# A sparse-attention and expert kernel on one core: a new written-out order, the first pair's block as one transfer, three table products on another engine

## The chip, the cores and the metric

The kernel runs on one core of a Trainium2 chip. The metric is the device time of one execution in microseconds (us), as the median of several runs: 202.86 us before the change (three runs, 202.06 to 202.98).

The core has five engines with a queue each: TensorE (PE in the profile, its weight loads PEld), VectorE (DVE), ScalarE (ACT), GpSimd (POOL) and SyncE (SP). SyncE issues nearly all DMA transfers here. Each engine works its own queue strictly in the order in which the program was written, and waits for the others by semaphores.

## The reference

Attention over 4 batches, 8 heads, 768 positions and 64 columns, followed by a soft mixture of 8 experts over the 3072 tokens. A position sees the first 8 keys and the 96 keys up to its own; the rest is masked, and a bias grows with the distance.

```python
scores = scale * np.matmul(q, k.transpose(0, 1, 3, 2))
keep = is_global | is_local
bias = -slopes[:, None, None] * dist[None, :, :]
scores = np.where(keep, scores + bias, -1000000000.0)
a = softmax(scores); x = np.matmul(a, v)          # x as (3072, 512)
...
logits = x @ phi                                  # 32 slots
d = softmax(logits, axis 0); slot_input = d.T @ x
slot_out[e] = np.maximum(slot_input[e] @ w1[e], 0) @ w2[e]
out = softmax(logits, axis 1) @ slot_out
```

(Softmax is written out in the reference, with a maximum taken off and 1e-9 added to each sum.)

## The kernel before

**Tiling.** A unit is one batch and a pair of heads: 16 units, numbered 0 to 15. Queries and keys of a unit come as one block of 128 partitions by 1664 values (832 KB, `load_qk`), its values as 448 KB (`load_v`). The 768 keys are cut into seven blocks of 120 with the 8 global keys ahead of each, and a block is multiplied with at most 216 queries, so that a score tile is keys by queries. The seven blocks go in three groups through two PSUM tiles: `scores(u, k)` writes tile (3u + k) modulo 2, for both heads.

**The steps of a unit.** `biased(u, k)` on VectorE (line 544) adds the bias table to a score tile, writes it to SBUF and keeps the running maximum. `max_t` and `max_r` (lines 551, 556) turn that into one number for the unit. `exponential(u, i)` on ScalarE (line 560) handles one head. The weights are then split into two 16-bit halves: `w_hi` (ScalarE, line 563) casts, and `w_lo` (line 570) subtracts the cast from the original, in three parts a head, either on GpSimd or, as `w_lo_dve`, on VectorE. The values are split the same way: `v_hi` on GpSimd (line 503), `v_hi_act` on ScalarE (506) or `v_hi_dve` on VectorE (509), and `v_lo` on VectorE (513). `values(u, i)` is 39 matmuls (line 587) of halves by halves. `ev_sums`, `ev_recs` and `ev_mul` divide by the row sums, `tr` transposes the result, `tr_copy` (ScalarE, 629) or `tr_copy_dve` (VectorE, 633) brings it to SBUF, and `logits` multiplies with phi. Every fourth unit ends a batch, with a few steps on its logits.

**The bias table.** The four head pairs need four tables of 1728 values in 16 bit. `table_even` (264), `table_odd` (268) and `table_rest` (273, three copies) make the first; `table_pair(p)` (280) makes table p by multiplying the first with 0.25 to the p. `biased(u, k)` of unit u reads table u modulo 4.

**The order.** Nothing is scheduled by the compiler. `ORDER` (line 51) is a list of steps written out by a planner, 608 of them, and lines 841 and 842 issue them one after the other. A step's place against others on the same engine is its place in that engine's queue. `warm` steps are matmuls on constants whose result nobody reads. The list also has the loads: `piece`, `extra` and `free` bring the experts' weights into ten tiles of their own, into gaps of the attention's tiles, and into those tiles as they come free.

```python
for name, u, *args in ORDER:
    steps[name](u, *args)
```

**Behind the attention.** `last_dispatch`, the two halves of the hidden layer (line 106), the projections (139) and the combination (199) run in a fixed order that is not in `ORDER`.

Of the kernel before, what the change touches and what calls it, by code (L numbers as in the profile page):

```python
# [15 lines left out]
AF = mybir.ActivationFunctionType  # L16
# [5 lines left out]
B, H, S, D = 4, 8, 768, 64  # L22
# [7 lines left out]
QW = KB + WIN  # L30
# [9 lines left out]
KW = NJ * KR  # L40
KCOL = tuple(KR * ((j + 5) % NJ) for j in range(NJ))
Q1 = KB + QW
# [9 lines left out]
NP = H // 2  # L52
# [157 lines left out]
class BiasTable:  # L210
# [58 lines left out]

    def rest(self):  # L270
        t = self.tabs[0]
        for at, n in ((2 * QW, QW), (3 * QW, QN[5]), (3 * QW + QN[5], QN[6])):
            self.nc.vector.tensor_copy(out=t[:, :, at:at + n], in_=t[:, :, QW:QW + n])

    def unit(self, p, k):

        return self.tabs[p][:, :, QW * k:QW * k + BW]

    def pair(self, p):
        self.nc.vector.tensor_scalar(out=self.tabs[p], in0=self.tabs[0], scalar1=0.25 ** p, scalar2=None, op0=ALU.mult)  # L280


@with_exitstack
def tile_attention_moe(ctx: ExitStack, tc: tile.TileContext, qk, v, phi, w1, w2, nn, out):
    nc = tc.nc
    const = ctx.enter_context(tc.tile_pool(name="const", bufs=1))
    fast = ExitStack()
    keep = fast.enter_context(tc.tile_pool(name="keep", bufs=1))
    wk = fast.enter_context(tc.tile_pool(name="wk", bufs=2))
    att = ExitStack()  # L290
    ap = att.enter_context(tc.tile_pool(name="ap", bufs=1))
    banks = ExitStack()
    psx = banks.enter_context(tc.tile_pool(name="psx", bufs=1, space=PSUM))
# [35 lines left out]
    rq = [r[:, 0:S + KW] for r in raws]  # L329
# [3 lines left out]
    def rqs(u):  # L333
        return EARLY[u][0][:, 0:S + KW] if u in EARLY else rq[u % 2]

    def vraws(u):
        return (EARLY[u][1] if u in EARLY else vt[:, VC * (u % 2):VC * (u % 2) + VC]).rearrange(by_head, j=NJ, i=2)
# [18 lines left out]
    held = []  # L356
    for name, i, *_ in ORDER:
        if name == "free":
# [4 lines left out]
    for k, n in enumerate(held):  # L363
        at = 0
        for c0, c1 in sorted(c for h, *cs in spaces for c in cs if h == n) + [(WP, WP)]:
            if at < c0:
                extras.append((NW + k, at, c0))
            at = c1
    places += places[0:5] + places[9:9 + 27 - npl]

    def piece(k):
        m, r = divmod(k, 16)
        if m == 0:
            a, r = divmod(r, 8)
            half, s = divmod(r, 4)
        else:
            half, r = divmod(r, 8)
            a, s = divmod(r, 4)
        return m, 4 * a + s, half
# [3 lines left out]
    def load_w(pieces, c0=0, c1=WP):  # L383

        for k in pieces:
            m, e, half = piece(k)
            nc.sync.dma_start(out=places[k][:, c0:c1], in_=(w1, w2)[m][e][:, WP * half + c0:WP * half + c1])

    def piece_of(k):
        load_w([k])  # L390

    def free(i):
        n, *cs = spaces[i]
        for c0, c1 in cs:
            load_w([NW + held.index(n)], c0, c1)

    FIRST = slice(KCOL[0], KW + Q1)

    def load_qk0(u):
        nc.sync.dma_start(out=rq[0][:, FIRST], in_=qk[0, 0][:, FIRST])  # L400

    def load_qk(u):
        for c in (slice(KW + Q1, KW + S), slice(0, KCOL[0])) if u == 0 else (slice(0, KW + S),):
            nc.sync.dma_start(out=rqs(u)[:, c], in_=qk[u // NP, u % NP][:, c])

    def load_v(u):
        nc.sync.dma_start(out=vraws(u), in_=v[u // NP, u % NP])

    def extra(i):
        if extras:  # L410
            k, c0, c1 = extras.pop(0)
            load_w([k], c0, c1)
# [28 lines left out]
    table = BiasTable(nc, tabs, xn01)  # L441
# [11 lines left out]
    def late_constants():  # L453
        nc.gpsimd.tensor_tensor(out=i4, in0=ident[:, 0:32], in1=ident[:, 32:64], op=ALU.add)
        nc.gpsimd.tensor_tensor(out=i4, in0=i4, in1=ident[:, 64:96], op=ALU.add)
        nc.gpsimd.tensor_tensor(out=i4, in0=i4, in1=ident[:, 96:128], op=ALU.add)
        nc.gpsimd.memset(sl, 0.0)
# [29 lines left out]
    class LeftBanks:  # L487

        n = 0
# [28 lines left out]
    def warm_x(u):  # L518
        for n in (256, 256, P):
            nc.tensor.matmul(out=xx[:, 0, 0:n], lhsT=idb[:, 0:P], rhs=idb[:, 0:n], start=True, stop=True)  # L520
# [301 lines left out]
    def table_even(u):  # L822
        table.even()

    def table_odd(u):
        table.odd()

    def table_rest(u):
        table.rest()

    def table_pair(p):
        table.pair(p)

    steps = dict(piece=piece_of, free=free, extra=extra, load_qk0=load_qk0, load_phis=load_phis, bcast=bcast, keys=keys, table_rest=table_rest, warm_x=warm_x, warm=warm,
                 table_even=table_even, table_odd=table_odd, table_pair=table_pair, load_qk=load_qk, load_v=load_v, v_hi=v_hi, v_hi_act=v_hi_act, v_hi_dve=v_hi_dve, v_lo=v_lo,
                 scores=scores, biased=biased, max_t=max_t, max_r=max_r, exponential=exponential, w_hi=w_hi, w_lo=w_lo, w_lo_dve=w_lo_dve, w_hi_dve=w_hi_dve,
                 values=values, ev_sum=ev_sum, ev_rec=ev_rec, ev_sums=ev_sums, ev_recs=ev_recs, ev_mul=ev_mul, tr=tr, tr_copy=tr_copy, tr_copy_dve=tr_copy_dve,
                 logits=logits, logits2=logits2, logits_half=logits_half, logits_all=logits_all, strip_max=strip_max, strip_exp=strip_exp,
                 strip_sum=strip_sum, by_token=by_token, by_token_copy=by_token_copy, lnat_copy=lnat_copy, dispatch=dispatch, dispatch_sum=dispatch_sum)
    late_constants()  # L840
    for name, u, *args in ORDER:
        steps[name](u, *args)
    left = LeftBanks()
    last_dispatch(left, lambda: warm_x(last))
    att.close()

# [287 lines left out]
```

## Time and profile before

| | us |
|---|---|
| median of three runs | 202.86 |
| the profiled execution, its own time | 204.56 |
| its span (first to last instruction) | 202.6 |
| TensorE busy in the span | 172.3 (85%) |
| VectorE busy | 156.6 (77%) |
| ScalarE busy | 123.2 (61%) |
| GpSimd busy | 101.0 (50%) |

The profiled execution is 1.70 us above the median. Its shares are averages over stages: an opening of some 15 us in which the first data come and the tables are made, the attention to about 142 us, the experts to about 188 us, and the last stores. GpSimd works in the attention alone. The page names engines and lines, and gives for each group of instructions the busy time, the mean of one, and what ended the idle time ahead of it. A busy TensorE is not one at its peak, since its matmuls are pipelined. The granted clock of TensorE is printed in tenths of full speed.

### The profile page before, as it was taken

Reading aid. Unit: us, or ns where it says so; the run is one execution under the profiler, and the core shown is the slowest. Engines: PE = TensorE matmul, PEld = TensorE weight load, DVE = VectorE, ACT = ScalarE, POOL = GpSimd, SP = SyncE. Lnnn points to the kernel's source line nnn. Section 1 sums busy time; section 2 is a strip of 40 time slices with the busy share of each in tenths; the row PEclk is TensorE's granted clock in tenths of the full one; section 3 lists DMA queues with packets and bytes.
Section 4 is the critical chain, followed back from the end, with each engine's and each line's share of the span. In section 5 each row is a group of like instructions: output and inputs, shape, how many; then the busy total and the mean of one; then the engine's idle time right before and its main releaser. Section 6 shows DMA issues by size and latency. Waiting matters only on the chain.

```text
span 202.6 us, 6321 instructions
## 1 busy us (share of the span) xinstructions
PE 172.3 (85%) x2609; PEld 126.9 (63%) x2609; DVE 156.6 (77%) x388; ACT 123.2 (61%) x157; POOL 101.0 (50%) x121
## 2 busy tenths in 40 slices
PE   7599989799988899979989896979799999998300
PEld 2365878698976679858768885764443355866300
DVE  6559999999999999999999999785786606634600
ACT  3018889879976788986997988733204421622400
POOL 6303999997779655696993999720000000000000
PEclk9969999999999999999999999999999999999855
DMA  5999999959999972770758779889979999496992
GB/s 180 294 424 408 409 408 390 343 177 390 357 408 417 408 269 100 262 250 12 261 197 296 220 199 318 303 314 330 421 269 387 417 417 417 181 306 218 328 335 78
DMA packets 18760, 61.38 MB, mean 303 GB/s; under 512 B 1570, under 2 KB 8994, under 8 KB 16546
## 3 DMA queue, kind: packets, MB, share of 16 engines
q1 hardware_dynamic: 18720, 60.89, 81.1%
q8 instruction: 22, 0.36, 0.7%
q14 instruction: 16, 0.13, 0.2%
q10 hardware_dynamic: 2, 0.00, 0.0%
HBM read 54.59 MB, written 6.29 MB: 300 GB/s over the span
## 4 chain that ended last, share of the span: by engine, by line


## 5 line engine op out<-in xcount | busy, mean ns | idle before, releaser
L570 POOL TENSOR_TENSOR ph<-tb,ph 128x432 f16<-128x432 f32 x78 | 86.8, 1145 | 30.4 <-ACT ph L563 30.0
L587 PE MATMUL x<-v,ph 128*128 128x65 f16 (+1 forms) x1248 | 43.4, 193 | 5.9 <-POOL ph L570 2.4
L587 PEld LDWEIGHTS <-ph 128*128 128x128 f16 x1248 | 41.2, 97 | 8.8 <-issue 3.8
L563 ACT CAST ph<-tb 128x1296 f16<-128x1296 f32 x32 | 40.3, 1271 | 10.0 <-PE x L587 8.6
L560 ACT ACTIVATE tb<-tb,nb 128x1296 f32<-128x1296 f32 x32 | 43.5, 1374 | 4.0 <-DVE nb L556 3.1
L535 PE MATMUL sc<-raw 64*128 64x216 f32 (+1 forms) x392 | 41.1, 346 | 4.0 <-DMA raw<-in_qk_dram 3.9
L535 PEld LDWEIGHTS sc<-raw 64*128 64x128 f32 x392 | 33.0, 192 | 11.6 <-issue 5.7
L544 DVE CUSTOM_DVE_ANT_1 tb<-sc,tt,mx 128x864 f32<-128x864 f32 x16 | 17.8, 1115 | 3.9 <-PE sc L535 3.2
L513 DVE SCALAR_TENSOR_TENSOR v<-vt,v 128x896 f16<-128x896 f32 x14 | 19.4, 1383 | 0.0
L612 DVE CUSTOM_DVE_ANT_1 xn<-x,rc 120x448 f32<-120x448 f32 x32 | 18.9, 620 | 0.5
L624 PE MATMUL m<-ident,xn 120*128 120x120 f32 x105 | 15.7, 276 | 1.9 <-DVE al L671 0.7
L570 DVE TENSOR_TENSOR ph<-tb,ph 128x432 f16<-128x432 f32 x18 | 16.2, 916 | 0.0
L624 PEld LDWEIGHTS m<-ident,xn 120*128 120x128 f32 x105 | 10.7, 141 | 5.9 <-issue 1.5
L506 ACT ACTIVATE v<-vt 128x896 f16<-128x896 f32 x7 | 6.6, 948 | 11.1 <-DMA vt<-in_v_dram 11.1
L139 PE MATMUL x<-wp,wp 128*32 128x256 f32 x96 | 10.7, 380 | 0.0
L106 PE MATMUL hp<-wp,sl 128*32 128x512 f32 x80 | 10.5, 594 | 0.0
L544 DVE CUSTOM_DVE_ANT_1 tb<-sc,xtt,mx 128x864 f32<-128x864 f32 x8 | 8.8, 1100 | 0.2 <-DVE mx L544 0.2
L544 DVE CUSTOM_DVE_ANT_1 tb<-sc,xta,mx 128x864 f32<-128x864 f32 x8 | 8.9, 1109 | 0.0
L544 DVE CUSTOM_DVE_ANT_1 tb<-sc,tt 128x864 f32<-128x864 f32 x8 | 8.4, 1046 | 0.1
L503 POOL TENSOR_SCALAR v<-vt 128x896 f16<-128x896 f32 x7 | 7.8, 1114 | 0.5 <-PE x L587 0.5
L139 PE MATMUL x<-ph,wp 128*32 128x256 f32 x32 | 7.3, 380 | 0.0
L139 PE MATMUL x<-tb,wp 128*32 128x256 f32 x32 | 7.2, 379 | 0.0
(208 smaller groups left out, 279.5 us busy)
## 6 DMA issues: line engine op xcount, KB each, us to landing
wp<-in_w_dram SPq DMA_DIRECT2D x11, 1024.0 KB, 11.4
raw<-in_qk_dram SPq DMA_DIRECT2D x13, 832.0 KB, 5.2
vt<-in_v_dram SPq DMA_DIRECT2D x14, 448.0 KB, 6.5
wp<-in_w_dram SPq DMA_DIRECT2D x10, 512.0 KB, 6.3
tb<-in_w_dram SPq DMA_DIRECT2D x4, 1024.0 KB, 8.4
raw<-in_w_dram SPq DMA_DIRECT2D x2, 1024.0 KB, 13.7
out_dram<-ph SPq DMA_DIRECT2D x4, 512.0 KB, 3.5
out_dram<-v SPq DMA_DIRECT2D x4, 512.0 KB, 7.0
```

The lines of the kernel that those rows point to most:

```text
L106: nc.tensor.matmul(out=hp[n][32 * s:32 * s + 32, :], lhsT=slv(a, c, s), rhs=w1(e, c // 2)[:, (c % 2) * DF + 512 * n:(c % 2) * DF + 512 * n ...
L139: nc.tensor.matmul(out=o[32 * s:32 * s + 32, 0:w], lhsT=ht[:, c, 32 * s:32 * s + 32], rhs=w2(4 * a + s, half)[:, c0 + c * w:c0 + c * w + w ...
L503: nc.gpsimd.tensor_scalar(out=vhi[u % 2][:, :, :, 0:D], in0=vraws(u), scalar1=V_SC, scalar2=0.0, op0=ALU.mult, op1=ALU.add)
L513: nc.vector.scalar_tensor_tensor(out=vlo[k].rearrange("p j i d -> p (j i) d"), in0=vraws(u).rearrange("p j i d -> p (j i) d"), scalar=V_SC ...
L535: nc.tensor.matmul(out=z[:, i, at:at + n], lhsT=r_[r, KCOL[j]:KCOL[j] + KR], rhs=r_[r, KW + KB * j:KW + KB * j + n], start=True, stop=True)
L544: nc.vector.tensor_tensor_reduce(out=tb(u)[:, :, BW * k:BW * k + BW], in0=sc[(3 * u + k) % 2][:, :, 0:BW], in1=table.unit(u % NP, k), scal ...
L560: nc.scalar.activation(out=t, in_=t, func=AF.Exp, bias=nbs[u], scale=T_SC)
L563: nc.scalar.copy(out=blocks(phi_[i])[:, :, 0:QW], in_=tb(u)[:, i].rearrange("p (s c) -> p s c", c=QW))
L570: (engine or nc.gpsimd).tensor_tensor(out=blocks(plo_[i])[:, c, 0:QW], in0=tb(u)[:, i].rearrange("p (s c) -> p s c", c=QW)[:, c], in1=bloc ...
L587: nc.tensor.matmul(out=x[:, (D + 1) * t:(D + 1) * t + d], lhsT=w[:, c:c + P], rhs=vv[:, j, i, 0:d], start=(z == 0), stop=(z == len(ops) - ...
L612: nc.vector.tensor_tensor_reduce(out=xnb[(u // 2) % 3][:, :, c:c + D], in0=xv[:, i, :, 0:D], in1=rcs.pop((u, i)).unsqueeze(2).to_broadcast ...
L624: nc.tensor.transpose(out=m[:, at:at + KB], in_=xnb[(u // 2) % 3][:, t, P * (p % 2):P * (p % 2) + P], identity=ident[0:KB, 0:KB])
```

## The change

`ORDER` is replaced as a whole by another list from the planner, whose model now takes the access that VectorE and GpSimd share as a lock held for an instruction. Its steps are the same but for these: `load_qk0`, which brought the first part of pair 0 (592 of its 1664 columns), is gone, and `load_qk(0)` brings the whole block in one transfer; the three `table_pair` become `table_pair_act` on ScalarE; `v_hi` is on GpSimd three times (units 0, 1, 6) instead of eight, on ScalarE eleven times instead of eight, on VectorE twice (units 7, 14) instead of never; `tr_copy_dve` comes six times instead of five; `warm` has 16 matmuls instead of 17. `w_lo` stays at 78 on GpSimd and 18 on VectorE, though not the same ones. The order of `free` differs, so some weights lie in other tiles.

In the new list the loads of pair 0, values 0, pair 1, values 1, values 3 and pair 2 stand ahead of everything; `table_rest` stands ahead of the first `biased`; and all ScalarE work on table products stands ahead of its first exponential.

The first stretch of the list, before and after, and the edited functions:

```diff
-ORDER = [('bcast', 0), ('keys', 0), ('extra', 4), ('extra', 5), ('load_qk0', 0), ('warm', 0, 2), ('scores', 0, 0), ('extra', 6), ('load_qk', 0),
-   ('table_even', 0), ('extra', 0), ('table_odd', 0), ('warm', 0, 3), ('scores', 0, 1), ('load_qk', 1), ('biased', 0, 0), ('load_v', 0), ('extra', 1),
-   ('v_hi_act', 0), ('load_qk', 2), ('table_rest', 0), ('warm', 0, 1), ('scores', 0, 2), ('biased', 0, 1), ('biased', 0, 2), ('table_pair', 1),
-   ('piece', 0), ('load_v', 1), ('warm', 0, 2), ('scores', 1, 0), ('warm', 0, 1), ('max_t', 0), ('max_r', 0), ('biased', 1, 0), ('exponential', 0, 0),
-   ('w_hi', 0, 0), ('exponential', 0, 1), ('scores', 1, 1), ('warm', 0, 3), ('scores', 1, 2), ('w_hi', 0, 1), ('table_pair', 2), ('load_qk', 3),
-   ('w_lo', 0, 0, 2), ('biased', 1, 1), ('w_lo', 0, 0, 0), ('table_pair', 3), ('w_lo', 0, 0, 1), ('biased', 1, 2), ('extra', 8), ('warm', 0, 2),
-   ('scores', 2, 0), ('warm', 0, 3), ('max_t', 1), ('w_lo', 0, 1, 1), ('biased', 2, 0), ('w_lo', 0, 1, 0), ('scores', 2, 1), ('max_r', 1),
-   ('v_hi_act', 1), ('exponential', 1, 0), ('scores', 2, 2), ('v_lo', 0), ('biased', 2, 1), ('values', 0, 0), ('w_hi', 1, 0), ('load_v', 2),
-   ('w_lo', 0, 1, 2), ('scores', 3, 0), ('w_lo', 1, 0, 0), ('values', 0, 1), ('w_lo', 1, 0, 2), ('v_lo', 1), ('biased', 2, 2),
...
+ORDER = [('load_qk', 0), ('load_v', 0), ('load_qk', 1), ('load_v', 1), ('load_v', 3), ('load_qk', 2), ('extra', 8), ('bcast', 0), ('load_qk', 3),
+   ('keys', 0), ('load_v', 2), ('extra', 1), ('table_even', 0), ('warm', 0, 6), ('scores', 0, 0), ('table_odd', 0), ('table_rest', 0),
+   ('scores', 0, 1), ('table_pair_act', 1), ('biased', 0, 0), ('v_hi', 0), ('biased', 0, 1), ('warm', 0, 2), ('scores', 0, 2), ('table_pair_act', 2),
+   ('biased', 0, 2), ('warm', 0, 1), ('scores', 1, 0), ('table_pair_act', 3), ('v_hi', 1), ('biased', 1, 0), ('warm', 0, 1), ('max_t', 0),
+   ('scores', 1, 1), ('max_r', 0), ('v_lo', 0), ('scores', 1, 2), ('exponential', 0, 0), ('biased', 1, 1), ('load_v', 4), ('w_hi', 0, 0),
+   ('extra', 0), ('load_phis', 0), ('biased', 1, 2), ('warm', 0, 5), ('scores', 2, 0), ('extra', 6), ('exponential', 0, 1), ('w_lo', 0, 0, 1),
+   ('extra', 5), ('biased', 2, 0), ('load_qk', 5), ('warm', 0, 1), ('max_t', 1), ('scores', 2, 1), ('load_qk', 4), ('w_lo', 0, 0, 0), ('w_hi', 0, 1),
+   ('max_r', 1), ('w_lo_dve', 0, 0, 2), ('scores', 2, 2), ('exponential', 1, 0), ('biased', 2, 1), ('w_lo', 0, 1, 0), ('values', 0, 0),
+   ('w_lo_dve', 0, 1, 1), ('scores', 3, 0), ('w_hi', 1, 0), ('w_lo_dve', 0, 1, 2), ('v_lo', 1), ('values', 0, 1), ('exponential', 1, 1),
+   ('w_lo', 1, 0, 0), ('biased', 2, 2),
...
@@ class BiasTable
-    def rest(self):
+    def rest(self, copy):
         t = self.tabs[0]
         for at, n in ((2 * QW, QW), (3 * QW, QN[5]), (3 * QW + QN[5], QN[6])):
-            self.nc.vector.tensor_copy(out=t[:, :, at:at + n], in_=t[:, :, QW:QW + n])
+            copy(out=t[:, :, at:at + n], in_=t[:, :, QW:QW + n])
...
+    def pair_act(self, p):
+        self.nc.scalar.activation(out=self.tabs[p], in_=self.tabs[0], func=AF.Copy, scale=0.25 ** p)
@@ def tile_attention_moe
-    FIRST = slice(KCOL[0], KW + Q1)
-
-    def load_qk0(u):
-        nc.sync.dma_start(out=rq[0][:, FIRST], in_=qk[0, 0][:, FIRST])
-
     def load_qk(u):
-        for c in (slice(KW + Q1, KW + S), slice(0, KCOL[0])) if u == 0 else (slice(0, KW + S),):
-            nc.sync.dma_start(out=rqs(u)[:, c], in_=qk[u // NP, u % NP][:, c])
+        nc.sync.dma_start(out=rqs(u), in_=qk[u // NP, u % NP])
...
     def table_rest(u):
-        table.rest()
+        table.rest(nc.vector.tensor_copy)
+
+    def table_rest_act(u):
+        table.rest(nc.scalar.copy)
+
+    def table_pair_act(p):
+        table.pair_act(p)
```

## Rows read from the trace of the kernel before

**Rows 1.** Stretches: window, length, busy us by engine, granted clock, DMA share, GB/s

```profile
15.33:129.30 113.97, 103.91 (x1836) 87.44 (x1835) 111.38 (x264) 97.67 (x109) 92.18 (x83) 1.00 0.80 297
148.00:188.00 40.00, 39.31 (x470) 21.68 (x467) 21.32 (x48) 13.45 (x24) 0.00 (x0) 1.00 0.85 322
```

**Rows 2.** VectorE's waits, 15 to 130 us: total us, times, longest

```profile
DVE m L556 <- PE m L551: 1.1, 1, 1.1
DVE tb L544 <- DVE mx L544: 0.5, 3, 0.2
DVE rsall L600 <- PE x L587: 0.2, 1, 0.2
DVE tb L544 <- DVE ph L570: 0.2, 1, 0.2
```

**Rows 3.** Timeline of VectorE, opening: start us, us, instruction, [idle before <- releaser]

```profile
6.35 0.27 DVE L268 TENSOR_SCALAR tt<-tt 128x432 bf16<-128x432 bf16 x1
6.77 1.06 DVE L544 CUSTOM_DVE_ANT_1 tb<-sc,tt 128x864 f32<-128x864 f32 x1
7.75 0.52 DVE L273 COPY tt<-tt 128x432 bf16<-128x432 bf16 x3
10.36 1.12 DVE L544 CUSTOM_DVE_ANT_1 tb<-sc,tt,mx 128x864 f32<-128x864 f32 x1 [2.08 <-PE sc L535]
12.56 1.12 DVE L544 CUSTOM_DVE_ANT_1 tb<-sc,tt,mx 128x864 f32<-128x864 f32 x1 [1.08 <-PE sc L535]
13.60 0.61 DVE L280 TENSOR_SCALAR tt<-tt 128x1728 bf16<-128x1728 bf16 x1
15.33 0.30 DVE L556 CUSTOM_DVE_ANT_0 m<-m,shift 128x128 f32<-128x128 f32 x1 [1.12 <-PE m L551]
```

**Rows 4.** Timeline of TensorE, opening (columns as in Rows 3)

```profile
5.62 1.00 PE L535 MATMUL sc<-raw 64*128 64x216 f32 x8 [1.12 <-DMA raw<-in_qk_dram]
9.32 1.00 PE L535 MATMUL sc<-raw 64*128 64x216 f32 x8 [1.96 <-DMA raw<-in_qk_dram]
```

**Rows 5.** Busy time by stretch, opening (columns as in Rows 1)

```profile
2.00:10.00 8.00, 4.83 (x27) 2.20 (x25) 5.27 (x20) 1.04 (x3) 4.29 (x25) 1.00 0.93 290
11.00:12.00 1.00, 1.00 (x8) 0.96 (x8) 0.48 (x2) 0.00 (x0) 0.00 (x0) 0.50 1.06 419
```

**Rows 6.** Instructions of lines 513 and 570: ns min/median/max, first and last start

```profile
L513 DVE SCALAR_TENSOR_TENSOR v<-vt,v x14: 1078/1090/1894, 20.8 to 131.1; 128x896 f16<-128x896 f32 x14
L570 POOL TENSOR_TENSOR ph<-tb,ph x78: 995/1012/1863, 18.5 to 132.8; 128x432 f16<-128x432 f32 x78
L570 DVE TENSOR_TENSOR ph<-tb,ph x18: 545/806/1417, 35.5 to 134.5; 128x432 f16<-128x432 f32 x18
```

**Rows 7.** The long stretch, line 513 alone, then line 570 alone

```profile
15.55:129.30 113.75, 20.80 (x15) 1.00 0.79 297
15.55:129.30 113.75, 14.59 (x15) 83.34 (x75) 1.00 0.79 297
```

**Rows 8.** Instructions of lines 503, 506, 563, 633 (columns as in Rows 6)

```profile
L503 POOL TENSOR_SCALAR v<-vt x7: 932/949/1462, 52.0 to 127.3; 128x896 f16<-128x896 f32 x7
L506 ACT ACTIVATE v<-vt x7: 937/949/953, 12.8 to 105.4; 128x896 f16<-128x896 f32 x7
L563 ACT CAST ph<-tb x32: 1255/1272/1277, 17.1 to 131.4; 128x1296 f16<-128x1296 f32 x32
L633 DVE COPY xtt<-m x1: 648/648/648, 60.1 to 60.1; 128x480 f32<-128x480 f32 x1
```

**Rows 9.** Timeline of ScalarE, opening (columns as in Rows 3)

```profile
12.80 0.95 ACT L506 ACTIVATE v<-vt 128x896 f16<-128x896 f32 x1 [9.75 <-DMA vt<-in_v_dram]
15.72 1.38 ACT L560 ACTIVATE tb<-tb,nb 128x1296 f32<-128x1296 f32 x1 [1.97 <-DVE nb L556]
```

**Rows 10.** Waits of ScalarE and GpSimd, 15 to 130 us (as Rows 2)

```profile
ACT ph L563 <- PE x L587: 8.6, 11, 2.2
POOL ph L570 <- ACT ph L563: 29.2, 13, 11.1
```

More of the change, by code (lines that the diff above doesn't have):

```diff
@@ L828, in table_rest @@
     def table_rest(u):
-        table.rest()
+        table.rest(nc.vector.tensor_copy)
[3 more added lines that the diff above has]
+        table.pair_act(p)
     def table_pair(p):
         table.pair(p)
-    steps = dict(piece=piece_of, free=free, extra=extra, load_qk0=load_qk0, load_phis=load_phis, bcast=bcast, keys=keys, table_rest=table_rest, warm_x=warm_x, warm=warm,
+    steps = dict(piece=piece_of, free=free, extra=extra, load_phis=load_phis, bcast=bcast, keys=keys, table_rest=table_rest, table_rest_act=table_rest_act, table_pair_act=table_pair_act, warm_x=warm_x, warm=warm,
                  table_even=table_even, table_odd=table_odd, table_pair=table_pair, load_qk=load_qk, load_v=load_v, v_hi=v_hi, v_hi_act=v_hi_act, v_hi_dve=v_hi_dve, v_lo=v_lo,
```

2 lines of the change are left out of this document (1 added, 1 removed).

## The prediction

> **What bounds the kernel now.** I read the stretches first [rows 1]. From 15.33 to 129.30 us, nearly all of the attention, VectorE is busy for 111.38 of 113.97 us; TensorE has 103.91, GpSimd 92.18, ScalarE 97.67. The reader is to see that one engine has no room and the next only 10 us (113.97 - 103.91). The list of what VectorE waited for in that time has four lines, 2.0 us together, and its first, 1.1 us, is the one at 15.33 [rows 2]. So behind 15.33 the attention ends when VectorE has worked off its queue. Ahead of 15.33 it has not enough to do: between the first `biased` at 6.77 and `max_r` at 15.33 it idles 2.08, 1.08 and 1.12 us, 4.28 in all [rows 3]. The first and longest gap is a transfer: the second group of scores stood until 9.32 for the rest of the first pair's queries and keys [rows 4]. The second comes with TensorE at the lower of its two levels: the granted clock is 0.50 (1.2 GHz) in the microsecond from 11, after an engine that had nothing from 7.4 to 9.3 [rows 5].
>
> A part of VectorE's 111.38 us is waiting inside instructions. `v_lo` takes 1078 ns at its shortest and 1894 at its longest, `w_lo` on VectorE 545 and 1417, `w_lo` on GpSimd 995 and 1863 [rows 6]. All read two tensors in SBUF. Fifteen of each lie in the stretch: 20.80 - 15 x 1.08 = 4.6 us and 14.59 - 15 x 0.545 = 6.4 us above the shortest, 11.0 us in sum [rows 7].
>
> From 148 to 188 TensorE is busy 39.31 of 40.00 us with the experts [rows 1]; nothing there is edited. It idles 0.69 us there, so no transfer holds it up, and the end moves with the attention's end.
>
> **The change part by part.** The sum is made against the profiled execution: span 202.6 us, own time 204.56, 1.96 around the span. It lies 1.70 above the median of 202.86; I carry the difference over.
>
> *The opening's transfers.* SyncE now issues the first pair's whole block (832 KB, 0.852 MB) first, then values 0, pair 1, values 1, values 3, pair 2. Before, 0.697 MB (two leftovers of weights and the first part of pair 0) were there at 5.62 [rows 4]. At the 290 GB/s of 2 to 10 us [rows 5] that much has moved at 2.0 + 2.4 = 4.4, so I add 1.2 us of lag. Pair 0 whole is then there at 2.0 + 2.9 + 1.2 = 6.1 us at that rate, and earlier at the 419 GB/s that the full rows reach at 11 us [rows 5]. The table's three copies now stand ahead of the first `biased`: 6.62, where the table's first half is written, plus 0.52 for the copies [rows 3] gives 7.14. Scores 0,0 take 1.00 us [rows 4] and are done at 7.1: no cost. Pair 1 is behind 2.16 MB: 8.4 us at 419 GB/s, 10.7 at 290; it is needed near 9.5. I take the full rows' rate, since these are full rows, and keep 1.2 us as the other end. What is pushed back on SyncE's queue is weights, read from 148 us on. Values 4 now stand in that queue behind a wait for `v_lo` 0; pairs 5 and 4 stand behind it, for scores more than 10 us later.
>
> *VectorE in the opening.* From 7.14: `biased` 0,0 to 8.2, 0,1 to 9.25. Scores 0,2 need the bank that 0,0 frees at 8.2 and take some 1.3 us with the wait's hop (1.00 for as many columns [rows 4]), so `biased` 0,2 starts at 9.7 (0.5 idle). `biased` 1,0 follows at 10.8, `max_r` 0 at about 11.9; behind it stand `v_lo` 0 and `biased` 1,1, whose scores are done by 12.1. I take 0.9 us of idle time (ends 0.5 and 3.5, the latter with late data and the low clock through the same instructions): 4.28 - 0.9 = 3.4 us gained.
>
> *The pair tables.* Three products of 0.61 us leave VectorE (one is in [rows 3]): 1.8 us gained. On ScalarE each costs about 1.62 us: 896 elements take 0.949 and 1296 take 1.271 [rows 8], so 1728 give 1.271 + 432 x 0.0008 (ends 1.3 and 3.2, twice that). Three from 7.2 end near 12.0. ScalarE idled 9.75 us until 12.80 before [rows 9], and its first exponential started at 15.72; now it waits for `max_r` 0 at 12.1. So the cover holds; without it, at 3.2 us each, the exponential would start at 16.8.
> The Trainium skill ("ScalarE: Activation LUTs", section "Rules for kernel authors") speaks against this edit: products belong on VectorE, up to three times faster in 16 bit. The ratio in the rows is 2.7. By the rule alone the edit would cost 3 x (1.62 - 0.61) = 3.0 us; I go by the idle 9.75 us.
>
> *What VectorE gets.* Two `v_hi` (units 7 and 14): the bounds are 0.61, a 16-bit product over about as many bytes [rows 3], and 1.08, `v_lo` over the same 896 elements [rows 6]. It reads one tensor, not two, but in 32 bit, so I take 0.8, between them: 1.6 us. One more `tr_copy_dve` of 480 elements, 0.65 [rows 8].
>
> *Waits at the shared access.* Thirty instructions pay the 11.0 us, 0.37 each. GpSimd loses seven `v_hi` of 0.95 inside the stretch [rows 8], 7% of its 92.18 us, which saves 0.8 in proportion; the two new `v_hi` on VectorE pay 0.7. I take zero. The new order could make it anything from 11 us less (all meet an idle GpSimd) to as much more (each pays the 0.82 or 0.87 between shortest and longest); nothing in the trace tells how the two queues will meet.
>
> *The drain* behind 129.30, where VectorE runs dry and the last unit goes through, has the same steps: 0. Its ends are -1 and +1, about one cast [rows 8].
>
> Sum: -3.4 - 1.8 + 1.6 + 0.65 + 0 = -3.0 us. Profiled time 201.6, median **199.9**. What is late next is still VectorE's queue, and behind it TensorE, which keeps its 10 us of room because the pace stays.
>
> **The rivals.**
> *A. The queues meet less.* VectorE's two-input instructions fall into GpSimd's pauses and the 11.0 us shrink by 4 to 7. For it: GpSimd waits 29.2 us for ScalarE in the stretch [rows 10], as long as the thirty instructions need (16.2 + 8.2 = 24.4). Against it: TensorE's 10 us of room is the floor, and a pause shifts with every small delay. Time: 193 to 196.
> The Trainium skill ("SBUF — State Buffer", section "SBUF: two separate sides") calls this access an exclusive lock for a whole instruction, the first comer blocking the other. The trace agrees [rows 6]: the longest `v_lo` is longer by 816 ns, less than one GpSimd instruction of 995. By that rule alone a plan that knows the lock could take away all 11 us.
>
> *B. The opening is not shorter.* Pair 1 comes at 10.7, the clock drops again under scores 0,2 and 1,0 as it did [rows 5], and VectorE idles 3.5 us instead of 0.9: 202.5. For it: 290 GB/s over eight microseconds [rows 5]. Against it: TensorE has no gap like 7.4 to 9.3 any more.
>
> *C. Slower: `v_lo` behind ScalarE.* Eleven units, not eight, now get `v_hi` from ScalarE, each queued behind exponentials and casts, and `v_lo` stands in VectorE's full queue right behind. The casts wait 8.6 us for TensorE already [rows 10], and ScalarE's load in the stretch rises by 2.8 us to 88%. If `v_lo` waits 0.6 us in each of eleven units, that is 6.6 us against a gain of 3.0: 206.5. It decides from 0.27 us per unit. For it: VectorE has no idle time to lose, so each wait is paid in full. Against it: before, no `v_lo` waited for the eight [rows 2].
>
> **How the numbers follow.** Forecast 42%, own range 198.0 to 201.6 (the opening's and `v_hi`'s ends). A 18%, B 17%, C 23%. Within 0.5% is what a measurement of this kernel can't tell from no change: 201.85 to 203.87. Faster: 42 + 18 + 5 of B = 65%. Same: 12 of B and 1 of C = 13%. Slower: 22%. The range for 8 in 10 takes the near part of A and of C: 195.3 to 204.8.
>
> **What would show it.** Right: first exponential near 12.1 us; VectorE's idle time between 6.6 us and `max_r` 0 near 0.9; its busy share behind that still 97%; sums of `v_lo` and `w_lo` above their shortest near 11 us; last weights unwaited. Wrong: a `biased` that waits for scores after 10 us (B); `v_lo` waiting for ScalarE (C); a sum at the shared access of 6 us or under (A), or above 15.

## The result, and the profile after

| | before | after |
|---|---|---|
| median, us | 202.92 (202.06 to 203.44, 4 runs) | 192.69 (191.98 to 193.59, 4 runs) |
| ratio | | 0.950, 95% interval 0.945 to 0.956 |
| profiled execution: own time, span | 204.56, 202.6 | 192.46, 190.6 |
| VectorE busy in the span | 156.6 | 148.2 |

The kernel became 10.2 us faster; 3.0 were forecast, with 195.3 as the low end. Line numbers of after are three lower than those of before from line 503 on (`v_lo` is L510, `w_lo` L567, `biased` L541, `max_r` L553); `pair_act` is L283.

Instructions of `v_lo` and `w_lo`, beside [rows 6]: ns min/median/max, first and last start.

```profile
L510 DVE SCALAR_TENSOR_TENSOR v<-vt,v x14: 1079/1084/1093, 12.3 to 118.2; 128x896 f16<-128x896 f32 x14
L510 DVE SCALAR_TENSOR_TENSOR v<-wp,v x2: 1085/1087/1089, 26.7 to 33.2; 128x896 f16<-128x896 f32 x2
L567 DVE TENSOR_TENSOR ph<-tb,ph x18: 595/606/1423, 16.9 to 122.9; 128x432 f16<-128x432 f32 x18
L567 POOL TENSOR_TENSOR ph<-tb,ph x78: 996/1010/1942, 15.3 to 121.5; 128x432 f16<-128x432 f32 x78
L506 DVE TENSOR_SCALAR v<-vt x2: 620/622/623, 61.2 to 111.2; 128x896 f16<-128x896 f32 x2
```

This is where the time went. All sixteen `v_lo` take 1.08 to 1.09 us; none waits. Before, the longest took 1894 ns. Above 1.08 for each `v_lo` and 0.60 for each `w_lo` on VectorE, before spends 10.9 us in these 34 instructions and after 2.5. That is the wait inside them, called "waits" from here on. It falls only on those that start while a GpSimd instruction is under way (with more than 0.05 us of it left): 24 of the 34 in before, 9 in after. The 10 and the 25 others take at most 0.02 us above 1.08 or 0.60.

Two `v_lo` of after, and GpSimd around them: start us, us, instruction, [idle before <- releaser].

```profile
33.19 1.08 DVE L510 SCALAR_TENSOR_TENSOR v<-wp,v 128x896 f16<-128x896 f32 x1
39.81 1.08 DVE L510 SCALAR_TENSOR_TENSOR v<-vt,v 128x896 f16<-128x896 f32 x1
```

```profile
34.03 4.98 POOL L567 TENSOR_TENSOR ph<-tb,ph 128x432 f16<-128x432 f32 x5 [1.49 <-ACT ph L560]
40.69 4.96 POOL L567 TENSOR_TENSOR ph<-tb,ph 128x432 f16<-128x432 f32 x5 [1.67 <-ACT ph L560]
```

Once a unit GpSimd has no work until ScalarE has cast the next unit's weights: here 1.49 and 1.67 us, up to 34.03 and 40.69. The `v_lo` starts inside that pause, and 0.84 and 0.88 of its 1.08 us are over when it ends.

VectorE's opening (beside [rows 3]) and ScalarE's (beside [rows 9]):

```profile
6.67 0.85 DVE L273 COPY tt<-tt 128x432 bf16<-128x432 bf16 x3
7.55 1.06 DVE L541 CUSTOM_DVE_ANT_1 tb<-sc,tt 128x864 f32<-128x864 f32 x1
8.77 1.12 DVE L541 CUSTOM_DVE_ANT_1 tb<-sc,tt,mx 128x864 f32<-128x864 f32 x1 [0.15 <-DVE mx L541]
12.14 0.29 DVE L553 CUSTOM_DVE_ANT_0 m<-m,shift 128x128 f32<-128x128 f32 x1
...
7.55 1.65 ACT L283 ACTIVATE tt<-tt 128x1728 bf16<-128x1728 bf16 x1 [4.50 <-DVE tt L273]
12.52 1.38 ACT L557 ACTIVATE tb<-tb,nb 128x1296 f32<-128x1296 f32 x1 [0.26 <-DVE nb L553]
```

`max_r` 0 starts at 12.14, forecast 11.9; the product takes 1.65 us on ScalarE, forecast 1.62; the first exponential starts at 12.52, forecast 12.1.

The attention of after as one stretch, and what waited in it (columns as in [rows 1] and [rows 2]):

```profile
12.10:114.40 102.30, 99.85 (x1767) 84.35 (x1763) 98.70 (x251) 96.31 (x107) 77.52 (x75) 1.00 0.86 316
```

```profile
POOL ph L567 <- ACT ph L560: 26.8, 18, 4.6
ACT ph L560 <- PE x L584: 2.2, 6, 0.7
```

TensorE is busy for 99.85 of 102.30 us, VectorE for 98.70. TensorE's room, the part of the stretch in which it is idle, is 2.5 us; from `max_r` 0 to `max_r` 15 of before it was 8.9 (100.6 of 109.5), and 10 in the longer stretch of [rows 1]. ScalarE's casts wait 2.2 us for TensorE, 8.6 in [rows 10].

### The profile page after: what moved, and what is told of

It reads as the page before. It is cut to its first block, busy times and chain, and to the rows that moved or that the text cites. A ratio compares the mean times of both kernels' runs of the same rounds, so it can differ in the third digit from the quotient of the medians.

```text
span 190.6 us, 6315 instructions
## 1 busy us (share of the span) xinstructions
PE 171.0 (90%) x2608; PEld 126.5 (66%) x2608; DVE 148.2 (78%) x388; ACT 129.4 (68%) x162; POOL 90.5 (47%) x116
## 4 chain that ended last, share of the span: by engine, by line
## 5 line engine op out<-in xcount | busy, mean ns | idle before, releaser
L567 POOL TENSOR_TENSOR ph<-tb,ph 128x432 f16<-128x432 f32 x78 | 82.3, 1085 | 28.6 <-ACT ph L560 26.8
L532 PE MATMUL sc<-raw 64*128 64x216 f32 (+1 forms) x392 | 39.4, 338 | 0.8 <-DVE mx L541 0.6
L532 PEld LDWEIGHTS sc<-raw 64*128 64x128 f32 x392 | 32.4, 186 | 5.8 <-DVE mx L541 2.1
L541 DVE CUSTOM_DVE_ANT_1 tb<-sc,tt,mx 128x864 f32<-128x864 f32 x16 | 17.8, 1114 | 1.0 <-POOL ph L567 0.4
L510 DVE SCALAR_TENSOR_TENSOR v<-vt,v 128x896 f16<-128x896 f32 x14 | 15.2, 1085 | 0.2
L567 DVE TENSOR_TENSOR ph<-tb,ph 128x432 f16<-128x432 f32 x18 | 13.2, 752 | 0.0
L541 DVE CUSTOM_DVE_ANT_1 tb<-sc,xtt,mx 128x864 f32<-128x864 f32 x8 | 8.9, 1111 | 0.5 <-PE sc L532 0.4
L541 DVE CUSTOM_DVE_ANT_1 tb<-sc,xta,mx 128x864 f32<-128x864 f32 x8 | 8.8, 1100 | 0.1
L503 ACT ACTIVATE v<-vt 128x896 f16<-128x896 f32 x9 | 8.6, 952 | 0.0
L541 DVE CUSTOM_DVE_ANT_1 tb<-sc,tt 128x864 f32<-128x864 f32 x8 | 8.4, 1054 | 0.1
L202 ACT COPY tt<-cp 128x512 f32<-128x512 f32 x4 | 2.4, 603 | 7.6 <-PE cp L199 7.1
L106 PEld LDWEIGHTS hp<-wp,sl 128*32 128x32 f32 x80 | 2.9, 110 | 6.6 <-issue 6.3
```

What stands on the lines that cost most here:

```text
L106: nc.tensor.matmul(out=hp[n][32 * s:32 * s + 32, :], lhsT=slv(a, c, s), rhs=w1(e, c // 2)[:, (c % 2) * DF + 512 * n:(c % 2) * DF + 512 * n ...
L503: nc.scalar.activation(out=vhi[u % 2][:, :, :, 0:D], in_=vraws(u), func=AF.Copy, scale=V_SC)
L510: nc.vector.scalar_tensor_tensor(out=vlo[k].rearrange("p j i d -> p (j i) d"), in0=vraws(u).rearrange("p j i d -> p (j i) d"), scalar=V_SC ...
L532: nc.tensor.matmul(out=z[:, i, at:at + n], lhsT=r_[r, KCOL[j]:KCOL[j] + KR], rhs=r_[r, KW + KB * j:KW + KB * j + n], start=True, stop=True)
L541: nc.vector.tensor_tensor_reduce(out=tb(u)[:, :, BW * k:BW * k + BW], in0=sc[(3 * u + k) % 2][:, :, 0:BW], in1=table.unit(u % NP, k), scal ...
L567: (engine or nc.gpsimd).tensor_tensor(out=blocks(plo_[i])[:, c, 0:QW], in0=tb(u)[:, i].rearrange("p (s c) -> p s c", c=QW)[:, c], in1=bloc ...
```

## The experiments

Four theories stand against each other in what follows. **S**: the new list puts VectorE's two-input instructions into GpSimd's pauses. **L**: GpSimd, with three `v_hi` in place of eight, is merely lighter. **O**: the other opening shifts the queues. **P**: a better-fed TensorE is what counts. The runs are compared with before on their own chip (median 202.5 to 203.0). This table is of the profiled executions, in us: attention is from `max_r` 0 to `max_r` 15, busy and idle are VectorE's in it.

| kernel | max_r 0 | attention | busy | idle | waits | span | median, runs |
|---|---|---|---|---|---|---|---|
| before | 15.3 | 109.5 | 107.0 | 2.5 | 10.9 | 202.6 | 202.92 |
| b0, before again | 13.0 | 108.9 | 106.5 | 2.4 | 10.3 | 200.0 | 202.36 |
| after | 12.1 | 102.3 | 98.7 | 3.6 | 2.5 | 190.6 | 192.69 |
| h1 | 12.8 | 108.4 | 104.3 | 4.1 | 9.7 | 199.4 | 200.22 |
| h2 | 13.5 | 106.7 | 101.5 | 5.3 | 4.3 | 196.3 | 198.71 |
| l1 | 12.0 | 107.0 | 102.7 | 4.3 | 8.0 | 196.6 | 198.30 |
| l2 | 13.2 | 110.6 | 108.3 | 2.3 | 10.4 | 200.6 | 203.49 |
| s1 | 11.7 | 112.9 | 104.9 | 8.0 | 8.3 | 201.5 | 204.49 |
| s3 | 11.7 | 113.5 | 104.3 | 9.2 | 7.0 | 201.4 | 202.43 |
| p1 | 12.4 | 105.2 | 101.3 | 3.9 | 3.0 | 193.7 | 196.37 |
| q1 | 12.0 | 103.0 | 99.0 | 4.0 | 2.7 | 191.0 | 192.88 |
| z1 | 11.8 | 102.9 | 97.8 | 5.1 | 2.7 | 190.8 | 192.91 |
| n0, after cut | 13.8 | 102.5 | 97.4 | 5.1 | 0 | 192.6 | 194.55 |
| n2, before cut | 14.0 | 100.3 | 97.6 | 2.7 | 0.6 | 191.3 | 193.98 |
| n1, s3 cut | 12.8 | 106.0 | 97.8 | 8.2 | 0.2 | 194.9 | 196.90 |
| n3, s1 cut | 14.0 | 105.1 | 98.0 | 7.2 | 0 | 195.1 | 196.97 |

**h1 and h2: the list in two halves.**

```diff
-ORDER = AFTER
+ORDER = AFTER[:59] + [what is left, in BEFORE's order]   # h1; h2: BEFORE[:59] + [what is left, in AFTER's order]
```

Of h1:

> The order of after up to and including max_r 1, then what is left in the order of before (with its engines for v_hi, w_lo and tr_copy). Theory S (the order puts VectorE's two-input instructions into GpSimd's pauses, and their waits go): the opening brings its own 5 us (max_r 1 comes 3.9 us earlier with v_lo 0 already done), the waits above the shortest v_lo and w_lo on VectorE stay near 10 us, time 196.5 to 199. Rival O (the opening shifts the phase of the two queues, and that alone clears the waits): waits under 4 us, 192 to 194. Rival P (an earlier and fuller start of TensorE and ScalarE is what counts, the waits are a side effect): 192 to 195 with the waits at 10.

Of h2:

> The order of before up to and including max_r 1 (with its parts of the first block and its products on VectorE), then what is left in the order of after. S: the opening's 5 us are not there, the waits of v_lo and w_lo on VectorE from unit 2 on fall to 3 us or less, time 195 to 198. O: waits near 10, 201 to 203. P: 200 to 203.

h1: ratio 0.988 [0.983, 0.992], 2.8 us, less than S expected; the waits stay at 9.7. O and P fall: an earlier start alone clears nothing. h2: 0.982 [0.976, 0.987], 4.3 us, with the waits at 4.3 (32 instructions here, since two more `w_lo` are GpSimd's). Of these, 2.1 are in units 0 and 1, and the 2.3 from unit 2 on are within S's 3; the time is a little above S's 198. The two halves make 7.1 of 10.2.

**l1 and l2: GpSimd's load.**

```diff
-('v_hi_act', 3) ... ('v_hi_dve', 7) ... ('v_hi_act', 15)
+('v_hi', 3) ... ('v_hi', 7) ... ('v_hi', 15)     # l1, on after: units 3, 5, 7, 10, 11, 13, 14, 15; l2, on before: the reverse
```

Of l1:

> After, with the eight v_hi that GpSimd had before given back to it, each at the same place in the list (GpSimd then has ten, ScalarE and VectorE lose six and two). S: v_hi fills part of the pauses that v_lo stands in, so that some v_lo wait, 2 to 4 us, less 1.2 us of v_hi on VectorE: 193 to 196. Rival L (GpSimd's lighter load is what cleared the waits): all of them come back, waits near 10 us, 200 or more. If places in the list count alone: 191 to 192.5.

Of l2:

> Before, with the eight v_hi of GpSimd given to ScalarE (six, each behind the second cast of the unit ahead, unit 5's behind an exponential) and VectorE (two, right ahead of their v_lo); nothing else moved. S: the places of v_lo are those of before, so waits fall by 2 us at most, which the two v_hi on VectorE (1.2 us) take back: 201.5 to 203.5. L: waits fall to 4 us or less: 195 to 198.

l1 (GpSimd has eleven `v_hi` in it, not ten): 0.978 [0.974, 0.983], 198.30, between the two expectations: 5.5 of the 8.4 us of waits come back. l2 (GpSimd has none, after has three): 1.004 [1.001, 1.008]; with GpSimd lighter than in after the waits are 10.4, where the two executions of before have 10.9 and 10.3, and the two `v_hi` on VectorE are added, so L falls. Neither half alone clears the waits: the places need the pauses, and `v_hi` on GpSimd filled some of them. In l1:

```profile
30.44 0.94 POOL L500 TENSOR_SCALAR v<-wp 128x896 f16<-128x896 f32 x1
31.34 1.97 POOL L567 TENSOR_TENSOR ph<-tb,ph 128x432 f16<-128x432 f32 x2
33.65 5.73 POOL L567 TENSOR_TENSOR ph<-tb,ph 128x432 f16<-128x432 f32 x5 [0.34 <-ACT ph L560]
```

```profile
33.70 1.91 DVE L510 SCALAR_TENSOR_TENSOR v<-wp,v 128x896 f16<-128x896 f32 x1
```

The `v_hi` at 30.44 takes up the pause, 1.49 us in after, to 0.34. GpSimd starts 0.05 us ahead of the same `v_lo`, which then takes 1.91 us.

**s1, s2, s3: `v_lo` moved by one `biased`.**

```diff
 ('w_hi', 3, 0),
-('v_lo', 3), ('values', 2, 1), ('exponential', 3, 1), ('w_lo', 3, 0, 2), ('biased', 5, 0),
+('values', 2, 1), ('exponential', 3, 1), ('w_lo', 3, 0, 2), ('biased', 5, 0), ('v_lo', 3),     # s3; s1: ahead of ('biased', 4, 2)
```

Of s1:

> After, with v_lo of units 1 to 9 and 12 to 14 one biased earlier in VectorE's queue (with the v_hi on VectorE that stands right ahead of it); same instructions, same engines. Theory S2 (the place of v_lo in GpSimd's pause, and the pause being free, together cleared the waits; the time follows the length of VectorE's queue): v_lo now meets the last w_lo of the unit ahead on GpSimd, 0.3 to 0.5 us each, v_lo in sum 4 to 6 us above after's 17.4, time 3 to 6 us above after: 196 to 199. Theory L2 (with 78 w_lo and 3 v_hi GpSimd is light enough, places don't matter): v_lo within 1 us of after's sum, 192 to 193.5.

Of s2:

> After, with v_lo of units 1 to 13 one biased later in VectorE's queue. S2: v_lo meets the first w_lo of its own unit, v_lo in sum 4 to 6 us above after's, and values may wait a little for the later v_lo: 196 to 199.5. L2: 192 to 193.5.

Of s3:

> After, with v_lo of units 1 to 13 one biased later in VectorE's queue, and the load that refills the tile it reads (units 7 to 14's values) kept right behind it. S2 (place and free pause together): v_lo meets the first w_lo of its own unit on GpSimd, 0.3 to 0.5 us each, v_lo in sum 3 to 6 us above after's 17.4, time 196 to 201. L2 (GpSimd is light enough, places don't matter): 192 to 193.5.

In s2 the loads of values 7 to 14 stand ahead of the `v_lo` that still needs the tile, so it waited for them and read later values; its 216.96 us says nothing on the question, and s3 keeps those loads behind. s1: 1.010 [1.007, 1.013]; s3: 0.998 [0.995, 1.002]. One `biased` earlier (twelve of the `v_lo`) or later (thirteen) takes the whole gain away, more than S2 expected, and L2 falls. Waits explain about half of the attention's 10.6 and 11.2 us: 5.8 and 4.5 us more than in after. VectorE's idle time grew by 4.4 and 5.6. In s3, between 12 and 126 us:

```profile
DVE m L553 <- PE m L548: 3.6, 5, 1.1
PE x L584 <- DVE xmax L609: 3.4, 4, 1.1
PE sc L532 <- DVE mx L541: 3.0, 2, 1.5
DVE tb L541 <- PE sc L532: 2.1, 3, 1.3
```

Two engines, each full in after, take turns in waiting for the other. Part of it comes with TensorE's clock, which in after stays at 1.00 all through the attention. In s1 the granted clock is 0.50 (1.2 GHz) from 68.4 to 71.8 us, behind 8.4 us in which TensorE was busy for 4.5; in s3 from 97.0 to 100.4, behind 7.0 us with 5.1. VectorE idles for 2.1 and 1.3 us in these stretches.

**n0 to n3: the access taken away.** Was that other half the access too? These kernels leave out most of the lower halves that GpSimd makes; nearly all of them stays zero.

```diff
-(engine or nc.gpsimd).tensor_tensor(out=blocks(plo_[i])[:, c, 0:QW], ...)        # two blocks of 216 columns
+nc.gpsimd.tensor_tensor(out=blocks(plo_[i])[:, c, 0:8], ...)                     # 8 columns of one block, GpSimd's w_lo only
+nc.gpsimd.memset(blocks(w)[:, :, 0:QW], 0.0)                                     # both tiles, once, at the start
```

Of n0:

> After, with each w_lo on GpSimd cut to the first 8 columns of one block (the rest of the lower halves stays zero; all waits and places stay). GpSimd then hardly holds the shared access. v_lo and w_lo on VectorE at their shortest. Both theories: 2.4 us of waits go, TensorE is full already: 189 to 192.

Of n1:

> The one with v_lo one biased later (s3), with the same cut of GpSimd's w_lo. If the access made the place matter, the waits and the idle time behind them: within 2 us of the cut after. If VectorE and TensorE wait for each other because the places no longer fit: 4 to 6 us above the cut after.

Of n3:

> The one with v_lo one biased earlier (s1), with the same cut of GpSimd's w_lo. Access: within 2 us of the cut after. Handshake: 4 to 6 us above it.

Of n2:

> Before, with the same cut of GpSimd's w_lo. Access: 11 us of waits go, and what stays between it and the cut after is the opening and the tables (1.1 and 1.8 us) less v_hi and tr_copy on VectorE (1.9): 190 to 194, within 2 us of the cut after. If the new list is better for other reasons than the access: 4 us or more above the cut after.

Ratios to before: n0 0.958 [0.953, 0.963], n2 0.960 [0.954, 0.965], n1 0.975 [0.969, 0.981], n3 0.975 [0.970, 0.980]. Without the access the list of before is as fast as that of after: 193.98 and 194.55. It gains 8.5 us by the cut. The cut also shortens GpSimd's own work, from 88.7 to 23.5 us of the attention, but that is not what pays: VectorE's busy time falls by 9.4 us and the attention by 9.2, while its idle time stays (2.5 and 2.7). The list of after gains nothing, where 189 to 192 was expected: n0 is 1.9 us above after. Its `max_r` 0 comes 1.7 us later (13.8): the first `biased` starts at 8.22 and not at 7.55, and the fourth waits 1.0 us for scores, with the granted clock at 0.50 from 10.2 to 13.7. Behind it the attention takes 102.5 us in one and 102.3 in the other. `v_lo` in n2:

```profile
L515 DVE SCALAR_TENSOR_TENSOR v<-vt,v x14: 1079/1086/1091, 19.5 to 120.4; 128x896 f16<-128x896 f32 x14
```

The moved kernels stay 2.4 us above n0, between the 2 us expected if the access is all and the 4 to 6 of a handshake, in the attention 3.5 (n1) and 2.6 (n3); s3 and s1 were 9.7 and 11.8 above after. So 2.4 us stay without the access, and the rest is the access and what its waits set off, the low clock among it: n1 and n3 have 1.00 all through the attention.

**p1, q1: the two named edits.**

```diff
-('table_pair_act', 1), ('biased', 0, 0), ... ('biased', 1, 0)
+('biased', 0, 0), ... ('table_pair', 1), ('biased', 1, 0)       # p1, also 2 and 3; q1: ('load_qk0', 0) and load_qk(0) in two parts, as before
```

Of p1:

> After, with the three products of the pair tables on VectorE again, each right ahead of the first biased that reads it. By the length of VectorE's queue: 3 x 0.6 us, 194.2 to 195 with the waits unchanged. If the later phase of the queue brings waits back: up to 2 us more, 197. If VectorE's queue is not what counts (TensorE is as full): within 0.8 us of after, 192 to 193.5.

Of q1:

> After, with the first pair's block in the three transfers of before, at the head of the list. If the one transfer is worth what the opening of before without its drop of the clock suggests: max_r 0 starts near 13 us, 0.9 later than in after, and the time is 193 to 194. If VectorE's queue takes it up, or the two later parts are there in time: 192 to 193. If it is worth the 3 us of the profiled opening of before: 195 to 196.

p1: 0.966 [0.961, 0.971], 3.7 us above after, where 1.8 was the sum by durations. Two of the products are longer than the 605 ns of the first, since GpSimd is at work:

```profile
L280 DVE TENSOR_SCALAR tt<-tt x1: 605/605/605, 10.7 to 10.7; 128x1728 bf16<-128x1728 bf16 x1
L280 DVE TENSOR_SCALAR xta<-tt x1: 1103/1103/1103, 15.9 to 15.9; 128x1728 bf16<-128x1728 bf16 x1
L280 DVE TENSOR_SCALAR xtt<-tt x1: 985/985/985, 24.0 to 24.0; 128x1728 bf16<-128x1728 bf16 x1
```

They make 2.7 us. The two start inside a GpSimd instruction, the first doesn't. With waits of 3.0 in place of 2.5 that is 3.1 us, the difference of the two spans; the 0.6 between this and the medians' 3.7 is not explained. q1: 0.952 [0.948, 0.956], the same as after; the one transfer is worth nothing that can be measured.

**b0: before once more.**

> Before, unchanged, for a second profiled execution. If the low clock of the first one's opening (0.50 near 11 us) is part of the kernel, it is there again and max_r 0 starts near 15.3 us. If it was that execution's, the granted clock stays at 1.00, max_r 0 starts at 13.2 to 13.5 us, as in the two experiments that kept this opening, and the execution is 1 to 2 us shorter than 204.56. The waits of v_lo and w_lo on VectorE near 11 us either way.

```profile
7.02 1.06 DVE L544 CUSTOM_DVE_ANT_1 tb<-sc,tt 128x864 f32<-128x864 f32 x1 [0.39 <-PE sc L535]
8.80 1.12 DVE L544 CUSTOM_DVE_ANT_1 tb<-sc,tt,mx 128x864 f32<-128x864 f32 x1 [0.28 <-PE sc L535]
10.12 1.12 DVE L544 CUSTOM_DVE_ANT_1 tb<-sc,tt,mx 128x864 f32<-128x864 f32 x1 [0.20 <-PE sc L535]
12.97 0.30 DVE L556 CUSTOM_DVE_ANT_0 m<-m,shift 128x128 f32<-128x128 f32 x1 [1.21 <-PE m L551]
```

```profile
11.00:12.00 1.00, 0.74 (x8) 0.69 (x8) 0.77 (x3) 0.00 (x0) 0.00 (x0) 1.00 1.09 402
```

The second `biased` comes 1.6 us earlier than in [rows 3], the clock stays at 1.00 where [rows 5] has 0.50, and `max_r` 0 starts at 12.97, not 15.33. The prediction's opening was one execution's: h2, l2 and w1, which share this opening, have 13.5, 13.2 and 13.9.

**z1: a version that might beat both.**

```diff
-('v_hi_dve', 7) ... ('v_hi_dve', 14)
+('v_hi_act', 7) ... ('v_hi_act', 14)     # each behind the second cast of the unit ahead
```

> After, with the two v_hi on VectorE (units 7 and 14) given to ScalarE, each behind the second cast of the unit ahead. By the length of VectorE's queue: 2 x 0.62 us off, 191.2 to 191.8. ScalarE has 1.9 us more, at 93% of the attention's time: if its casts come late by as much, or the places of v_lo in the pauses shift, 193 to 196.

0.954 [0.950, 0.957], as fast as after, where 191.2 to 191.8 was expected by the length of VectorE's queue. VectorE's attention is 0.9 us shorter in work and 1.5 longer in idle time: its longest wait is 1.7 us for TensorE's `values`, and TensorE was busy for 97.6% of the stretch in after. Work taken off VectorE no longer pays here. ScalarE has 1.6 us more to do in z1; that this plays no part is not shown.

**w1: a shorter hold.** On before:

```diff
-c = slice(2 * part, 2 * part + 2)
+for c in (slice(2 * part, 2 * part + 1), slice(2 * part + 1, 2 * part + 2)):     # GpSimd's w_lo only
```

> Before, with each w_lo on GpSimd as two instructions of one block each in place of one of two. If the loser waits for the end of the other engine's whole instruction: the longest v_lo falls from 1.89 us to about 1.6, the longest w_lo on VectorE from 1.42 to about 1.1, their waits in sum from 10 us to 5 or 6, time 197 to 200 unless GpSimd's 78 extra starts make it late (then 203 to 208). If the two engines share the access bit by bit and slow each other down: the longest stay within 0.1 us of before's, time 202.5 to 204.

One run took 204.16 us, five took 209.84 to 211.97, so no ratio is given; the five lie above every expectation. The longest `w_lo` on VectorE fell from 1417 to 1068 ns, as for a hold of one instruction. But the waits sum to 14.7 us, 8.2 of them in one `v_lo` of the profiled execution, which is one of the five:

```profile
30.34 9.32 DVE L513 SCALAR_TENSOR_TENSOR v<-wp,v 128x896 f16<-128x896 f32 x1
```

```profile
17.09 18.50 POOL L571 TENSOR_TENSOR ph<-tb,ph 128x216 f16<-128x216 f32 x30 [9.74 <-ACT ph L563]
35.57 0.93 POOL L503 TENSOR_SCALAR v<-wp 128x896 f16<-128x896 f32 x1
36.47 2.23 POOL L571 TENSOR_TENSOR ph<-tb,ph 128x216 f16<-128x216 f32 x4
```

GpSimd works without a gap from 17.09 to 38.70. A `v_lo` that starts at 30.34 ends at 39.66, 0.96 us behind that run: it got its turn only when GpSimd had nothing left, after fourteen GpSimd instructions that had started behind it. This happened once; no other of the 34 is more than 0.73 us above 1.08 or 0.60. How the runs without a profile came to their times is not shown.

## Why the prediction was wrong

**The step that failed is "Waits at the shared access ... I take zero".** It measured -8.4 us (10.9 to 2.5). The text held that "nothing in the trace tells how the two queues will meet". Trace and list did hold a hint. Each new `v_lo` stands behind GpSimd's last `w_lo` of the unit ahead and in front of its own unit's first, where GpSimd pauses; 13 of before's 16 do not. The hint is weak by itself, since 7 of these 13 wait in before and one of the other three does. But half of before's `v_lo`, with a median of 1090 in [rows 6], already took no wait, and the new list came from a planner that knows the lock: zero, with as much to either side, left both out. n2 shows that it is the access: without it both lists take the same time. So rival A happened, beyond its own 4 to 7 us and 193 to 196: 8.4 and 192.69. It had been given 18%.

**The bound.** Right for before: VectorE is busy for 107.0 of the attention's 109.5 us, and each kernel that lengthened its queue (l1, p1, l2) grew by about as much. "TensorE, which keeps its 10 us of room because the pace stays" was wrong with the waits: the pace rose and the room went, from 8.9 to 2.5 us, and z1 finds no more to gain on VectorE.

**The opening.** Against the profiled execution it came as forecast: `max_r` 0 3.2 us earlier, VectorE's gaps between 6.6 and 12.14 about 0.35 us in place of 0.9. That agreement is luck: it is with one execution's opening. b0 starts `max_r` 0 at 12.97, and h2, l2 and w1 at up to 13.9, so 0.8 to 1.8 us were there to be had. Of the 4.28 us of idle time b0 has 2.1 (0.39, 0.28, 0.20 and 1.21), and the rest, with the later data and the low clock, was the profiled execution's own. The median of 202.9 beside an own time of 204.56 was the hint, and "I carry the difference over" passed it by. q1 shows that the transfers had no part in what remained.

**The tables**: 1.62 us each on ScalarE was right (1.63 to 1.65), and the cover held. On VectorE they took 0.60 to 0.61 each in before, 1.8 in all, as forecast. p1's 3.7 is what they cost in the queue of after, where two of them meet GpSimd. **`v_hi` on VectorE** took 0.62, not 0.8, each; **`tr_copy_dve`** 0.65 as forecast.

**The sum, against the profiled span**: VectorE's busy time changed by -8.4 waits - 1.8 tables + 1.2 `v_hi` + 0.65 copy = -8.35 (the page: 156.6 to 148.2, -8.4); its opening gaps by 0.35 - 4.28 = -3.9; together -12.3, the span -12.0. On medians it is -10.2; b0's opening is the shorter one, and the span from b0 to after is -9.4.

**B** did not come: no `biased` waits for scores beyond 0.4 us. **C** did not: none of the sixteen `v_lo` waits for ScalarE.

The Trainium skill ("SBUF — State Buffer", section "SBUF: two separate sides") has the access locked by whoever starts first, for a whole instruction, with the other blocked. l1's 1.91 us and w1's shorter `w_lo` agree. w1's 9.32 us goes beyond it: a blocked instruction can lose many turns in a row, here fourteen.

## What to carry to other kernels

Where a trace has instructions of one form at two durations, treat the difference as a wait with a place: find the other engine's pauses and check, step by step in the new list, whether the instruction falls into them; don't carry the mean over. An edit that looks small can move it out of them (s1, s3). Before an opening's idle time goes into a sum, look whether the profiled execution stands at the median and whether the clock in it is at the level of the other runs. When one full engine gets lighter, check which engine is then the next: here TensorE's room fell from 8.9 to 2.5 us.

## What the runs showed of the hardware

- A VectorE instruction at the shared access can be passed over by GpSimd's back-to-back instructions: 9.32 us for one of 1.08 (w1, once).
- Two-input instructions of VectorE wait there when they start inside a GpSimd instruction, and in these kernels not otherwise: 24 of 34 in before, with 10.9 us of waits, and 9 in after, with 2.5.
- One-input instructions of VectorE can pay there too: table products of 16 bit 1.10 and 0.99 us beside a busy GpSimd, 0.605 alone (p1); `v_hi` 1.07 in s1, 0.62 in after.
- The opening's clock differs between executions of one kernel: 0.50 near 11 us in one of before, 1.00 in the other, and 2.4 us between their `max_r` 0.
